# Fences between value steps as empty GpSimd instructions, and six instead of four bit transfers ahead of the first pair's fence

## The chip, the cores and the metric

The kernel runs on one core of a Trainium2 chip. The core has five engines with queues of their own: TensorE (PE, with its weight loads shown apart as PEld), VectorE (DVE), ScalarE (ACT), GpSimd (POOL) and SyncE (SP, which here only issues transfers). The metric is the device time of one execution in microseconds. Before the change it is 868.96 us, the median of three runs (868.72 to 869.63).

## What is computed

The reference is an attention with a mask from hashes, and behind it a feed-forward block. Cut to what matters:

```python
# q, k, v: (4, 8, 768, 64); proj: (64, 6); all float32
q_bucket = sum(((q @ proj) > 0) * 2**arange(6))      # six sign bits make a bucket; k the same
scores = where(q_bucket == k_bucket, q @ k.T / 8, -1e9)
attn = exp(scores - max) / (sum + 1e-9)
x = (attn @ v)                                        # brought to (3072, 512)
out = relu(x @ w_in)**2 @ w_out                       # 512 -> 2048 -> 512
```

Every query sees the keys whose six hash bits agree with its own.

## The kernel before

The kernel has an attention phase, up to about 320 us, and a feed-forward phase behind it (a fast product scheme by sums of blocks, with its weight sums prepared during the attention phase). The change touches the attention phase alone.

The 32 heads are worked off as 16 pairs, `for pr in range(NP)`. Two heads lie side by side on the 128 partitions, 64 each. The order of all instructions is written out by hand: on each engine the instructions run in the order in which the program names them.

For each pair the 768 keys are cut in six tiles `kt` of 128, and the 768 queries in two halves `i`. `score(pr, kt, i)` makes the scores of a key tile with a query half: `products` multiplies first the bits (`marks`), then the features, into one PSUM tile `st` (line 430), eight matmuls of 64 x 64; `weight` takes the exponential on ScalarE into a ring of four tiles `e` (line 436). A bit that differs subtracts so much that the exponential vanishes, which does the masking. `attend(pr, kt, s)` multiplies the weights with the values (`value`, line 486) and accumulates into `xo` in PSUM. `add_up` sums the weights on VectorE (line 473), and `sum_up` sums these over partitions with a matmul against ones (line 535). A step is one `score` and one `attend`; there are twelve in a pair, with `sum_up` and the hash products of the next pair (`hash_bits`, line 360) once in each.

The products with values are split by key halves (the upper and lower 64 rows of a key tile, multiplied side by side), and each `attend` has a parameter `s`: with `s` = 0 the first key half is multiplied with query half 0 and the second with query half 1, with `s` = 1 the other way round. Each query half has a PSUM block of its own, so at every change of `s` two key halves exchange the block into which they accumulate, and what the one has begun there must be finished before the other goes on. This is what `part(before, after)` does, the fence: a GpSimd instruction that waits for the last product before the change, and for which the first products behind the change wait. It is called in `attend` where `s` changes, and in `sum_up` between its halves: four times in an ordinary pair, ahead of `attend(pr, 0, 1)`, of `attend(pr, 2, 0)`, of `attend(pr, 4, 1)` (which runs in the next pair's turn) and of the second half of `sum_up`.

The instruction before the change is a write of one element into a tile `token` in SBUF (line 481). It waits for PE's semaphore, and, since all fences write the same element, for the write before it.

GpSimd also issues the transfers of the hash bits. `hash_bits` makes the products with `proj` for the next pair, `signs` and `weigh` turn them into signs and weights on ScalarE (tile `signed`), and `place_bits` (line 396) moves them to the partitions where `products` needs them, in eight transfers of 5.2 KB: four parts of (keys or queries, half), with two heads each. `PARTS` is the order of the parts: keys 0, queries 0, queries 1, keys 1. All eight are issued together behind `attend(pr, 0, 1)`, except for the first pair: there two parts are issued at that place, and the other two behind `attend(0, 2, 0)`, and so behind this one's fence on GpSimd's queue.

VectorE also converts weights for the feed-forward phase meanwhile, one piece a pair: `part_power` (line 151), `part_top` (lines 177 and 181), `round_weight` (lines 195 and 198), `sum_in` (line 594). `features` (line 344) transposes the next pair's queries and keys on VectorE.

The call of `place_bits` in the loop, ahead of `score(pr, 3, 1)`:

```python
            attend(pr, 0, 1)
            if more:
                place_bits(pr + 1, PARTS if pr else PARTS[:2])
```

Of the kernel before, what the change touches and what calls it, by code (L numbers as in the profile page):

```python
# [8 lines left out]
FP32 = mybir.dt.float32  # L9
# [25 lines left out]
def kernel(  # L35
# [10 lines left out]
    nc = tc.nc  # L46
# [50 lines left out]
    const = first.enter_context(tc.tile_pool(name="const", bufs=1))  # L97
# [11 lines left out]
    def spare(name):  # L109

        return ps_t.tile([P, 2, 512], FP32, name=name, tag="spare")
# [180 lines left out]
    def load_pair(pr):  # L292


        b, j = divmod(pr, PB)
        both = p_qk.tile([P, 2, S], FP32, name="qk_nat")
        for w, src in enumerate((q, k)):
            for g in range(4):
                h, e = divmod(g, 2)
                nc.sync.dma_start(  # L300
                    out=both[g * 32:(g + 1) * 32, w].rearrange("i (c d) -> i c d", d=32),
                    in_=src[b, 2 * j + h].rearrange("(c i) (e d) -> e i c d", i=32, e=2)[e],
                )
        nat[pr, "qk"] = both
# [36 lines left out]
    def features(pr):  # L341

        feat[pr] = p_f.tile([P, 2, S], FP32, name="feat")
        nc.vector.transpose(
            out=feat[pr].rearrange("p w s -> p (w s)"),
            in_=nat.pop((pr, "qk")).rearrange("p w s -> p (w s)"),
        )
# [39 lines left out]
    PARTS = (1, 0), (0, 0), (0, 1), (1, 1)  # L387

    def place_bits(pr, parts=PARTS):

        t = all_bits[pr % 2]
        for w, c in parts:
            bits[pr, w] = t[:, w]
            at = (2 * w + c) * NR_B
            for h in range(2):
                nc.gpsimd.dma_start(  # L396
                    out=t[h * D:h * D + NBITS + 1, w, c * HS:(c + 1) * HS],
                    in_=signed[at:at + NBITS + 1, h],
                )

    def first_keys(c, banks):

        if c == 0:
            bits[0, 1] = all_bits[0][:, 1]
        t = bits[0, 1]
        hash_bits(0, banks, (1,), (c,))
        at = slice((2 + c) * NR_B, (3 + c) * NR_B)
        cut = slice(c * HS, (c + 1) * HS)
        for h in range(2):
            nc.vector.tensor_scalar(  # L410
                out=t[h * D:h * D + NR_B, cut], in0=banks[at, h, 0:HS],
                scalar1=0.0, scalar2=None, op0=ALU.is_gt,
            )
        nc.vector.tensor_scalar(
            out=t[:, cut], in0=t[:, cut], scalar1=spans, scalar2=bases, op0=ALU.mult,
            op1=ALU.add,
        )
# [22 lines left out]
    def score(pr, kt, i, st=None):  # L440

        own = [feat[pr][:, w] for w in range(2)]
        marks = [bits[pr, w] for w in range(2)]
        st = st or turn("st")
        products(st, i, kt, marks, True)
        products(st, i, kt, own, False)
        weight(pr, kt, i, st)

    def first_score():

        own = [feat[0][:, w] for w in range(2)]
        marks = [bits[0, w] for w in range(2)]
        sts = [turn("st") for _ in range(2)]
        for i, st in enumerate(sts):
            products(st, i, 0, own, True)
        for i, st in enumerate(sts):
            products(st, i, 0, marks, False)
            weight(0, 0, i, st)
# [14 lines left out]
            nc.vector.tensor_tensor(out=totals[pr], in0=totals[pr], in1=e, op=ALU.add)  # L473

    SYNC = mybir.DependencyInfo(mybir.DependencyClass.Sync, mybir.DependencyReason.DATA)
    token = const.tile([1, 1], FP32, name="token")

    def part(before, after):


        step = nc.gpsimd.memset(token, 0.0)  # L481
        tc.add_manual_dep(step.ins, before.ins.name, SYNC)
        tc.add_manual_dep(after.ins, step.ins.name, SYNC)

# [7 lines left out]
    def attend(pr, kt, s):  # L492


        if (kt, s) == (0, 0):
            outs[pr] = ps_o.tile([P, 2, 512], FP32, name="xo")
        for r in range(2):
            for h in range(2):
                done = value(
                    pr, kt, slice(r * HK, (r + 1) * HK), h, (r + s) % 2,  # L500
                    (kt, s) == (0, 0), (kt, s) == (SB - 1, 1),
                )
                if turned.get(pr, s) != s:
                    part(lasts[pr], done)
                turned[pr] = s
        lasts[pr] = done
# [151 lines left out]
    with tc.manual_schedule():  # L658
# [21 lines left out]
        for pr in range(NP):  # L680
            more, old = pr + 1 < NP, pr - 1

            def beside(kt, s):
                if pr > 0:
                    attend(old, kt, s)

            if pr + 2 < NP:
                load_pair(pr + 2)
            if more and pr > 0:
                features(pr + 1)  # L690
            if pr == 0:
                first_score()
                first_keys(1, spare("hash"))
            else:
                score(pr, 0, 0)
                attend(old, 4, 0)
                score(pr, 0, 1)
                attend(old, 5, 0)
                add_up(old, SB - 1)
                if pr == 1:  # L700
                    part_top(0)
                round_weight(old)
                if later:
                    later.pop(0)()
                if more:
                    load_weight(pr + 1)
                for m in sums.get(pr, ()):
                    sum_in(m)
            score(pr, 1, 0)
            beside(4, 1)  # L710
            score(pr, 1, 1)
            beside(5, 1)
            if pr == 0:
                features(1)
            else:
                keep_x(old)
                sum_up(old, 0)
                if more:
                    hash_bits(pr + 1, turn("hash"))
                    signs(pr + 1)  # L720
                else:
                    score(pr, 2, 0)
                sum_up(old, 1)
                invert(old)
            add_up(pr, 1)


            if pr in (X_0 + 1, X_0 + 2):
                load_unit(pr - X_0 - 1)
            part_power(pr)  # L730
            if pr == 0:
                attend(pr, 0, 0)
            if more:
                score(pr, 2, 0)
            if pr > 0:
                spread(old)
                attend(pr, 0, 0)
            else:
                attend(pr, 1, 0)
            score(pr, 2, 1)  # L740
            if pr > 0:
                attend(pr, 1, 0)
                if more:
                    weigh()
                else:
                    place_power(pr, 0, 0)
            else:
                hash_bits(1, turn("hash"))
                signs(1)
            score(pr, 3, 0)  # L750
            if pr > 0:
                place_power(pr, 0, int(not more))
            else:
                weigh()
            attend(pr, 0, 1)
            if more:
                place_bits(pr + 1, PARTS if pr else PARTS[:2])
            score(pr, 3, 1)
            attend(pr, 1, 1)
            add_up(pr, 2)  # L760
            if pr > 0:
                normalize(old)
                if more:
                    place_power(pr, 0, 1)
                else:
                    place_power(pr, 1, 0)
            add_up(pr, 3)
            if more:
                load_values(pr + 1)


            score(pr, 4, 0)
            if more:
                place_power(pr, int(pr > 0), 0)
            else:
                place_power(pr, 1, 1)
            attend(pr, 2, 1)
            score(pr, 4, 1)
            if more:
                place_power(pr, int(pr > 0), 1)  # L780
            attend(pr, 3, 1)
            if 0 < pr < NP - 1:
                part_top(pr)
            score(pr, 5, 0)
            if pr == 0:
                place_power(0, 1, 0)
            if more:
                attend(pr, 2, 0)
            if pr == 0:
                place_bits(1, PARTS[2:])  # L790
            if 2 * PB < pr <= 2 * PB + NFT:
                load_x(0, slice(pr - 2 * PB - 1, pr - 2 * PB))
            score(pr, 5, 1, spare("st") if not more else None)
            attend(pr, 3, 0)
            if pr == 0:
                place_power(0, 1, 1)
            add_up(pr, 4)
        pr = NP - 1
# [810 lines left out]
```

## Time and profile before

| what | value |
|---|---|
| median of three runs | 868.96 us |
| the profiled execution | 869.21 us |
| its span (first to last instruction) | 867.3 us |
| PE busy | 854.5 us, 99% |
| DVE busy | 749.5 us, 86% |
| ACT busy | 361.9 us, 42% |
| POOL busy | 183.1 us, 21% |
| mean TensorE clock granted | 0.997 |
| writes of `token` on POOL | 62, together 14.6 us |
| bit transfers issued by POOL | 120, together 61.5 us |

Busy time is the time in which an engine had an instruction in work. In a row of the timeline stand the start, the duration, the engine, the line, the operation with what it writes and reads, and the count of instructions that were merged into the row; in brackets the idle time ahead of it and what ended it. In a row of a line or a tile stand the least, the median and the largest duration in ns. Weight loads (PEld) run ahead of the matmuls that use them, so that an idle PEld need not cost any time.

### The profile page before, as it was taken

How to read it: one execution, taken by the hardware profiler on the slowest of the kernel's cores; microseconds unless marked ns; L12 is line 12 of the kernel's file. 1: busy time of each engine (PE TensorE's matmuls, PEld its weight loads, DVE VectorE, ACT ScalarE, POOL GpSimd, SP SyncE). 2: the span in 40 equal slices, each digit the busy share in tenths (PEclk: the TensorE clock that was granted, in tenths of full speed). 3: DMA queues.
4: the chain of work that ended last, by engine and by line, in shares of the span. 5: the costliest groups of instructions: out<-in, count | busy, mean ns of one | idle time of the engine just before them, and what ended most of it. 6: DMA issues, size and time to landing. Idle time of an engine off the chain costs nothing.

```text
span 867.3 us, 16734 instructions
## 1 busy us (share of the span) xinstructions
PE 854.5 (99%) x6548; PEld 520.4 (60%) x6548; DVE 749.5 (86%) x1005; ACT 361.9 (42%) x648; POOL 183.1 (21%) x346
## 2 busy tenths in 40 slices
PE   8999999999999999999999999999999999999996
PEld 3544444444444444444788865557888655568885
DVE  5799999999999988998779978888889688888875
ACT  5787777788877752222111123332111233321110
POOL 1332222223322201652132111112000111100002
PEclk9999999999999999999999999999999999999998
DMA  9677899879998527999788865537758645355565
GB/s 206 127 139 151 177 176 203 192 168 249 249 222 223 167 68 258 319 308 298 279 287 258 187 158 175 171 112 254 260 150 189 158 168 170 117 167 160 147 182 100
DMA packets 226629, 168.03 MB, mean 194 GB/s; under 512 B 167112, under 2 KB 184848, under 8 KB 226544
## 3 DMA queue, kind: packets, MB, share of 16 engines
q1 hardware_dynamic: 187744, 87.19, 40.9%
q0 software_dynamic: 16416, 41.95, 15.7%
q10 hardware_dynamic: 22384, 37.76, 14.6%
q8 instruction: 53, 0.87, 0.4%
q14 instruction: 32, 0.26, 0.1%
HBM read 124.52 MB, written 41.68 MB: 192 GB/s over the span
## 4 chain that ended last, share of the span: by engine, by line
PE 96%; DMA 2%; DVE 1%; issue 0%; ACT 0%; POOL 0%; POOLq 0%; DVEq 0%; ACTq 0%
PE acc L837 39%; PE st L430 18%; PE acc L1056 16%; PE xo L486 14%; PE acc L1009 6%; PE tot L535 2%; PE hash L360 1%; DMA leaf<-w_out 1%; DMA bits<-signed 1%; PE xo L337 0%; DVE total L473 0%; PE tp L320 0%; POOL bits L396 0%; DVE bits L410 0%; ACT feat L327 0%
## 5 line engine op out<-in xcount | busy, mean ns | idle before, releaser
L436 ACT ACTIVATE e<-st 128x768 f32<-128x768 f32 x192 | 155.4, 810 | 62.4 <-PE st L430 59.2
L430 PE MATMUL st<-feat 64*64 64x384 f32 x1536 | 158.1, 483 | 1.0 <-DVE feat L329 1.0
L486 PE MATMUL xo<-e,v_nat 64*64 64x385 f32 (+1 forms) x1520 | 158.7, 485 | 0.0
L837 PE MATMUL acc<-b,leaf 128*128 128x256 f32 x600 | 133.4, 379 | 0.3 <-DMA leaf<-w_out 0.3
L837 PEld LDWEIGHTS acc<-b,leaf 128*128 128x128 f32 x600 | 113.6, 190 | 17.2 <-issue 1.4
L473 DVE TENSOR_TENSOR total<-total,e 128x1536 f32<-128x1536 f32 x64 | 111.8, 1746 | 4.4 <-ACT e L436 2.8
L486 PEld LDWEIGHTS xo<-e,v_nat 64*64 64x64 f32 (+1 forms) x1520 | 56.4, 133 | 69.9 <-issue 52.8
L1056 PE MATMUL acc<-t_x,w_unit 128*128 128x512 f32 x192 | 90.2, 592 | 0.0
L430 PEld LDWEIGHTS st<-feat 64*64 64x64 f32 x1536 | 57.3, 133 | 38.1 <-issue 33.5
L837 PE MATMUL acc<-t,leaf 128*128 128x256 f32 x336 | 76.2, 380 | 0.0
L837 PEld LDWEIGHTS acc<-t,leaf 128*128 128x128 f32 x336 | 63.7, 190 | 9.1 <-DVE t L594 0.5
L921 DVE SCALAR_TENSOR_TENSOR b<-h 128x512 f32<-128x512 f32 x96 | 65.7, 691 | 3.0
L430 PE MATMUL st<-bits 64*64 64x384 bf16 x768 | 65.8, 325 | 1.1 <-DMA bits<-signed 1.0
L396 POOL DMA_DIRECT2D bits<-signed x120 | 61.5, 520 | 23.2 <-ACT signed L385 22.8
L1056 PE MATMUL acc<-x,w_unit 128*128 128x512 f32 x128 | 60.1, 592 | 0.0
L481 POOL MEMSET token<- 1x1 f32 x62 | 14.6, 236 | 206.0 <-PE xo L486 155.9
L837 PE MATMUL acc<-x,w_unit 128*128 128x512 f32 x128 | 56.5, 593 | 0.0
L1056 PEld LDWEIGHTS acc<-t_x,w_unit 128*128 128x128 f32 x192 | 36.5, 190 | 28.9 <-issue 26.8
L837 PE MATMUL acc<-b_t,leaf 128*128 128x256 f32 x240 | 53.8, 379 | 0.0
L1154 POOL DMA_DIRECT2D out_dram<-h x26 | 16.8, 654 | 174.1 <-DVE h L1147 167.1
L874 POOL DMA_DIRECT2D raw_qk<-in_q_dram x32 | 17.3, 541 | 162.4 <-DVE peaks L878 162.4
L837 PEld LDWEIGHTS acc<-b_t,leaf 128*128 128x128 f32 x240 | 45.5, 190 | 6.2
(156 smaller groups left out, 1206.6 us busy)
## 6 DMA issues: line engine op xcount, KB each, us to landing
leaf<-w_out ACTq DMA_DIRECT2D x142, 256.0 KB, 3.2
w_unit<-w_in SPq DMA_DIRECT2D x16, 640.0 KB, 4.0
raw<-in_moe_w_in_dram SPq DMA_DIRECT2D x8, 1024.0 KB, 6.8
raw<-in_moe_w_out_dram SPq DMA_DIRECT2D x8, 1024.0 KB, 7.4
w_unit<-w_in SPq DMA_DIRECT2D x8, 896.0 KB, 8.6
w_out<-sums POOLq DMA_DIRECT2D x16, 448.0 KB, 7.9
sum<-w_in SPq DMA_DIRECT2D x16, 448.0 KB, 5.0
v_nat<-in_v_dram SPq DMA_DIRECT2D x16, 384.0 KB, 5.3
```

Source lines behind the costliest of these rows:

```text
L396: nc.gpsimd.dma_start(out=t[h * D:h * D + NBITS + 1, w, c * HS:(c + 1) * HS], in_=signed[at:at + NBITS + 1, h],)
L430: nc.tensor.matmul(out=st[k * HK:(k + 1) * HK, h, 0:HS], lhsT=src[1][rows, key], rhs=src[0][rows, cut], start=first, stop=not first, skip_ ...
L436: nc.scalar.activation(out=key_of(pr, kt)[:, :, i, 0:HS], in_=st[:, :, 0:HS], func=ACTF.Exp, scale=scale)
L473: nc.vector.tensor_tensor(out=totals[pr], in0=totals[pr], in1=e, op=ALU.add)
L486: return nc.tensor.matmul(out=outs[pr][h * D:(h + 1) * D, c, 0:HS + 1], lhsT=nat[pr, "v_nat"][rows, h, kt * D:(kt + 1) * D], rhs=key_of(pr ...
L535: done = nc.tensor.matmul(out=spares[pr][g * 32:(g + 1) * 32, c2, 0:QS], lhsT=ones[rows], rhs=totals[pr][rows, h, c, c2 * QS:(c2 + 1) * QS ...
L837: nc.tensor.matmul(out=acc[to], lhsT=a(i), rhs=b(i), start=first and i == 0, stop=last and i == n - 1, skip_group_check=True,)
L874: nc.gpsimd.dma_start(out=raw_qk[i][:, w], in_=flat[:, i * n:(i + 1) * n])
L921: nc.vector.scalar_tensor_tensor(out=out, in0=h, scalar=0.0, in1=h, op0=ALU.max, op1=ALU.mult)
L1009: nc.tensor.matmul(out=out, lhsT=w[:, a], rhs=b, start=start, stop=stop, skip_group_check=True)
L1056: nc.tensor.matmul(out=acc[to], lhsT=w[:, PLACE[a], f], rhs=bt[b](f), start=first and f == 0, stop=last and f == NFT // 2 - 1, skip_group_ ...
L1154: queue.dma_start(out=out[at, m0 + a * 32:m0 + (a + 1) * 32].rearrange("(c i) j -> i c j", i=32), in_=ot[a * 32:(a + 1) * 32].rearrange("i ...
```

## The change

The fence becomes an empty GpSimd instruction (`nop`) with the same two dependences, and the tile `token` goes. For the first pair, three of the four parts of the bits (six transfers) are issued at the earlier place instead of two (four transfers), so that one part remains behind the fence of `attend(0, 2, 0)`.

```diff
     SYNC = mybir.DependencyInfo(mybir.DependencyClass.Sync, mybir.DependencyReason.DATA)
-    token = const.tile([1, 1], FP32, name="token")
 
     def part(before, after):
-        step = nc.gpsimd.memset(token, 0.0)
+        step = nc.gpsimd.nop()
         tc.add_manual_dep(step.ins, before.ins.name, SYNC)
         tc.add_manual_dep(after.ins, step.ins.name, SYNC)
...
             attend(pr, 0, 1)
             if more:
-                place_bits(pr + 1, PARTS if pr else PARTS[:2])
+                place_bits(pr + 1, PARTS if pr else PARTS[:3])
             score(pr, 3, 1)
...
                 attend(pr, 2, 0)
             if pr == 0:
-                place_bits(1, PARTS[2:])
+                place_bits(1, PARTS[3:])
```

In the built program the empty instruction is a semaphore step of GpSimd's sequencer with a semaphore of its own. Five of the eight bit transfers of each later pair get one more semaphore step ahead of them (a wait for matmuls that read the same bits tile two pairs earlier). On the other engines the order of the instructions is as before.

## The prediction

> **What bounds the kernel now.** I read the page first (busy time, the chain that ended last, the costliest groups), then the answers for the tile `token` and for line 396, then the timeline around single fences, at last the busy time of each engine over whole pairs.
>
> ```profile
> PE 854.5 (99%) x6548; PEld 520.4 (60%) x6548; DVE 749.5 (86%) x1005; ACT 361.9 (42%) x648; POOL 183.1 (21%) x346
> ...
> PE 96%; DMA 2%; DVE 1%; issue 0%; ACT 0%; POOL 0%; POOLq 0%; DVEq 0%; ACTq 0%
> ...
> L481 POOL MEMSET token<- 1x1 f32 x62 | 14.6, 236 | 206.0 <-PE xo L486 155.9
> L481 POOL MEMSET token<- x62: 88/89/563, 17.5 to 314.5; 1x1 f32 x62
>   PEld xo L486: 16.7, 45
> ```
>
> PE is the bound: 99% busy, 96% of the chain. POOL is on the chain for under half a per cent, so 14.6 us of one-element writes say nothing yet. What matters is only where a late fence made PE start late. The third and fourth rows already show the oddity: 62 writes of one element take from 88 to 563 ns. The last row says that weight loads for value products waited 16.7 us for them; weight loads run ahead of the products, so most of that may be free.
>
> The timeline tells which fences are not free. A step of the attention phase is a group of score products and then a group of value products; its length is the distance from one `st<-bits` row to the next.
>
> ```profile
> 44.02 0.33 PE L430 MATMUL st<-bits 64*64 64x384 bf16 x4
> 44.82 0.82 PE L486 MATMUL xo<-e,v_nat 64*64 64x385 f32 x8
> 45.47 0.33 PE L430 MATMUL st<-bits 64*64 64x384 bf16 x4
> 45.62 0.69 DVE L177 TENSOR_SCALAR top<-raw 128x1024 uint32<-128x1024 uint32 x1
> 45.81 0.54 POOL L481 MEMSET token<- 1x1 f32 x1 [0.17 <-PE xo L486]
> 46.40 0.21 PEld L486 LDWEIGHTS xo<-e,v_nat 64*64 64x64 f32 x8 [0.62 <-POOL token L481]
> 46.40 0.88 PE L486 MATMUL xo<-e,v_nat 64*64 64x385 f32 x8
> 47.09 0.34 PE L430 MATMUL st<-bits 64*64 64x384 bf16 x4
> 48.55 0.34 PE L430 MATMUL st<-bits 64*64 64x384 bf16 x4
> ```
>
> 44.02 to 45.47 is 1.45 us, 47.09 to 48.55 is 1.46, but 45.47 to 47.09 is 1.62: this step lost 0.17 us. The fence between the two value groups began at 45.81 and ended at 46.35, and the products behind it started at 46.40. The vector operation of line 177 ran from 45.62 to 46.31, so the write ended just behind it.
>
> This is the fence in front of `attend(pr, 2, 0)`, the second of four in each pair. The other three cost nothing:
>
> ```profile
> 39.53 0.69 DVE L151 TENSOR_SCALAR power<-raw 128x1024 uint32<-128x1024 uint32 x1
> 39.65 0.33 PE L430 MATMUL st<-bits 64*64 64x384 bf16 x4
> 39.98 0.27 POOL L481 MEMSET token<- 1x1 f32 x1 [3.88 <-PE xo L486]
> 40.31 0.30 PEld L486 LDWEIGHTS xo<-e,v_nat 64*64 64x64 f32 x8 [0.35 <-POOL token L481]
> 41.11 0.33 PE L430 MATMUL st<-bits 64*64 64x384 bf16 x4
> ...
> 51.79 0.09 POOL L481 MEMSET token<- 1x1 f32 x1 [5.45 <-PE xo L486]
> 51.94 0.15 PEld L486 LDWEIGHTS xo<-e,v_nat 64*64 64x64 f32 x4 [0.17 <-POOL token L481]
> ...
> 285.79 0.09 POOL L481 MEMSET token<- 1x1 f32 x1 [3.35 <-PE tot L535]
> ```
>
> The first fence took 0.27 us, also ending with a vector operation (39.53 + 0.69 = 40.22 against 40.25), yet its step is 39.65 to 41.11, the usual 1.46: 0.33 us from the start of the write to the weight load is absorbed. The third took 0.09. The fourth (in front of the second half of the sums, line 535) takes 0.09 as well (285.79). The stall returns in each of the pairs 1 to 14; the last:
>
> ```profile
> 293.79 0.33 PE L430 MATMUL st<-bits 64*64 64x384 bf16 x4
> 295.24 0.33 PE L430 MATMUL st<-bits 64*64 64x384 bf16 x4
> 295.58 0.53 POOL L481 MEMSET token<- 1x1 f32 x1 [0.17 <-PE xo L486]
> 296.87 0.34 PE L430 MATMUL st<-bits 64*64 64x384 bf16 x4
> ```
>
> 1.45 us, then 1.63. The total fits: 14 writes of 0.54, 14 of 0.28 and 34 of 0.09 make 14.5 of the 14.6 us. Pairs 0 and 15 have none of the long ones.
>
> **The change part by part.** *Removed: 62 writes; added: 62 empty instructions.* In the built program an empty instruction is one step of POOL's sequencer: it waits for PE and counts up a semaphore of its own, for which PE then waits. It touches no memory. The trace has no such row; nearest are POOL's own semaphore steps and the short writes.
>
> ```profile
> L396 POOLq EVENT_SEMAPHORE  x16: 17/17/43, 21.8 to 289.8; - x16
> L396 POOL DMA_DIRECT2D bits<-signed x120: 512/518/674, 22.5 to 294.9; - x120
>   PE st L430: 1.0, 1
> DMA to landing us min/median/max: 1.5/3.7/5.9
> ...
> 22.46 2.22 POOL L396 DMA_DIRECT2D bits<-signed  x4 [4.91 <-ACT signed L385]
> 25.28 0.09 POOL L481 MEMSET token<- 1x1 f32 x1 [0.60 <-PE xo L486]
> 25.42 0.16 PEld L486 LDWEIGHTS xo<-e,v_nat 64*64 64x64 f32 x4 [0.16 <-POOL token L481]
> 25.76 2.05 POOL L396 DMA_DIRECT2D bits<-signed  x4 [0.39 <-issue]
> 29.02 0.66 PE L430 MATMUL st<-bits 64*64 64x384 bf16 x4 [0.99 <-DMA bits<-signed]
> 41.55 4.09 POOL L396 DMA_DIRECT2D bits<-signed  x8 [1.29 <-ACT signed L385]
> ```
>
> Lower end 0.02 us, upper end 0.09, the write at 51.79 that nothing disturbed. Both ends give the same sum, since even 0.27 (39.98) cost PE nothing: the stall of 0.17 goes whole. 14 x 0.17 = 2.4 us. The other 48 fences give nothing, because there PE is hidden from them by the score products that it still has in hand; without that cover the first fence would cost up to 0.17 us a pair today. What is late next at this place: nothing, the products are in order behind the score products of 45.47.
>
> Why the write took 0.54 us has two readings: the vector operation beside it, or the eight transfers whose descriptors POOL had just finished. The fence at 39.98 had no transfers before it since 27.81 (25.76 + 2.05) and still ended with the vector operation, so I take the first. The Trainium skill says the same in "SBUF — State Buffer", section "SBUF: two separate sides": VectorE and GpSimd share one port pair as an exclusive lock, and the one that comes second waits for the whole instruction. By that rule an instruction without memory never waits and the sum is the 2.4 us above; by the other reading an empty instruction could still be held behind the transfers, and the sum would be 0.
>
> *Waits added to the transfers.* The write counted as POOL's own work, and the transfers behind it took over its knowledge of PE's progress; the empty instruction counts apart, so five of the eight transfers of each pair get a semaphore step of their own ahead of them, for PE products of two pairs ago, long done. Queued behind them on POOL is the second fence, and PE behind that. Price: 5 x 0.02 us = 0.1 at the least, if none overlaps; the upper end is 5 x 0.09 = 0.45.
>
> Four transfers without such steps took 2.05 us (0.51 each); eight with two such steps among them took 4.09, also 0.51 each. So they hide under the 0.5 us of a transfer, and I take 0. Even the 0.45 would put the end of the eight from 45.64 to 46.09, still ahead of today's 46.35.
>
> *Six transfers ahead of the first pair's fence instead of four.* Two transfers (the queries' second half) move from behind the fence of 25.28 to 24.68, where the first four end; they are issued 1.08 us earlier, and the last two then also come 1.08 us earlier, at 25.70. Past the fence the order on POOL is otherwise the same, no other queue is touched. Gain: PE waits for bits once, 0.99 us at 29.02, but that is for the first four, which stay where they are; the two moved ones were not waited for (`PE st L430: 1.0, 1` is the only wait for any of them). Loss: the fence is queued behind two more transfers, 25.70 instead of 25.28 if it must wait for their end, and PE's weight load of 25.42 with it. That would cost at most what the later fence at 46.40 costs, 0.17 us, once. Whether a sequencer step waits for the end of POOL's work ahead of it isn't in these rows. In the Trainium skill's "PSUM — Partial Sum Buffer", section "Engine vs sequencer instructions", a sequencer waits only until earlier instructions are handed to the engine; by that the fence is on time and the cost 0. I take 0 and keep 0.17.
>
> The first four share engines with two more in flight, so their landing may shift either way. In the chain it is one row:
>
> ```profile
> 23.65 5.23 DMA bits<-signed
> ```
>
> At the slowest landing of any such transfer, 5.9 us, PE would start 0.7 us later; at the best the whole wait goes, 1.0 us. The moved ones stand behind the four in the same queue, so I take 0 between −1.0 and +0.7.
>
> **The sum.** The profiled execution took 869.21 us for a span of 867.3. 869.21 − 2.4 = 866.8; it stands 0.25 above the median of the three runs, so 868.96 − 2.4 gives 866.5.
>
> **The rivals.** *VectorE takes the gain.* In these pairs it is nearly as full as PE:
>
> ```profile
> core 0: us, PE busy (x) PEld busy (x) DVE busy (x) ACT busy (x) POOL busy (x), PEclk, DMA share, GB/s
> 189.73:208.95 19.22, 19.22 (x304) 9.06 (x288) 18.91 (x19) 14.96 (x24) 5.71 (x14) 1.00 0.95 237
> 208.95:228.16 19.21, 19.21 (x304) 9.09 (x288) 18.39 (x18) 14.96 (x24) 5.64 (x14) 1.00 1.01 241
> ```
>
> A pair of 19.21 us becomes 19.04. The ordinary pair needs 18.4 of VectorE, every third 18.9: both still fit, with 0.1 us to spare in the worst. If VectorE held all fourteen pairs at 19.21, the time would stay 868.96; if it held three pairs as full as the first row, 0.5 comes back: 867.0.
>
> *The empty instruction is no cheaper.* If it is held behind the transfers as the second reading has it, 868.96. Against it speaks 39.98.
>
> *The added waits slow POOL's queue: slower.* The second fence stands behind them. Its place today is 46.35; each transfer slower by d moves it to 45.64 + 5d. It decides from 5d = 0.7, that is 0.14 us a transfer. At 0.25 the fence would be at 46.89, 0.54 us behind today's in each of 14 pairs: 868.96 + 7.6 = 876.5. Steps of 17 to 43 ns speak against it, and the equal pace of 0.51.
>
> *The first pair's transfers land otherwise.* 865.5 with the whole wait gone, 867.2 with 0.7 more.
>
> **How the numbers follow.** Full gain with the first pair as it is: 0.58, 866.5, own range 866.0 to 867.1. First pair better as well: 0.09. First pair worse: 0.08, half of it still under 867.2. VectorE or the empty instruction keep most of the gain: 0.17, 867.3 to 869.2. Slow queue: 0.08. What a measurement of this kernel can tell is about 0.2%, 1.7 us, so faster means below 867.2: 0.58 + 0.09 + 0.04 = 0.71; within 0.2% 0.04 + 0.17 = 0.21; slower 0.08. The range 865.3 to 868.9 holds the first three cases and most of the fourth.
>
> **What would show it.** The step behind the second fence is 1.45 us in pairs 1 to 14, a pair from sum fence to sum fence is 19.04, no weight load of the value products waits 0.6 us for a fence. The eight transfers still take 4.1 us. In pair 0 the products at 25.73 are on time, and PE's wait at 29.02 is about 1 us. Wrong would be: a fence answered later than 46.1 in its pair, pairs still at 19.21 with VectorE without a pause, or a later landing of the first four bits.

## The result and the profile after

The kernel after takes 866.67 us (median; 865.79 to 868.13), beside 869.27 us for the kernel before on the same chip: a ratio of 0.9971, 95% interval 0.996 to 0.9982. The forecast was 866.5. Beside the last experiments it was measured again: 867.05 against 869.64, ratio 0.9973 (0.9961 to 0.9984). Both times the change is worth 2.6 us. The profiled execution took 866.6 us.

From the page of the kernel after: span, busy times, and the chain that ended last.

```profile
span 864.4 us, 16743 instructions
PE 851.6 (99%) x6548; PEld 519.3 (60%) x6548; DVE 749.3 (87%) x1005; ACT 362.3 (42%) x648; POOL 169.4 (20%) x284
...
PE 95%; DMA 2%; DVE 1%; issue 0%; POOL 0%; ACT 0%; POOLq 0%; DVEq 0%; ACTq 0%
```

POOL lost 13.7 us of work and its 62 writes. PE's busy time fell by 2.9 us though it does the same products: before, the stalls counted as busy (19.21 of 19.21 us in a pair).

The answers for line 480 (the fence, now a step of POOL's sequencer) and for the transfers:

```profile
L480 POOLq EVENT_SEMAPHORE  x62: 17/17/17, 17.0 to 311.2; - x62
  PEld xo L485: 7.8, 44
L396 POOL DMA_DIRECT2D bits<-signed x120: 515/521/677, 22.0 to 291.9; - x120
L396 POOLq EVENT_SEMAPHORE  x87: 17/17/43, 21.4 to 290.4; - x87
```

A fence takes 17 ns everywhere, and weight loads wait 7.8 us for it where they waited 16.7 us for the write. The transfers have 87 semaphore steps instead of 16, and a transfer takes 521 instead of 518 ns.

The timeline at the fence that the prediction was about:

```profile
43.40 0.33 PE L430 MATMUL st<-bits 64*64 64x384 bf16 x4
44.85 0.33 PE L430 MATMUL st<-bits 64*64 64x384 bf16 x4
45.01 0.69 DVE L177 TENSOR_SCALAR top<-raw 128x1024 uint32<-128x1024 uint32 x1
45.34 0.14 PEld L485 LDWEIGHTS xo<-e,v_nat 64*64 64x64 f32 x4 [0.18 <-POOLq L480]
46.30 0.33 PE L430 MATMUL st<-bits 64*64 64x384 bf16 x4
```

The same vector operation runs from 45.01 to 45.70 beside the fence, and the weight load starts at 45.34, in the middle of it. The step is 44.85 to 46.30, 1.45 us, where it was 1.62.

Two whole pairs, each as long as from one sum fence to the next (the same two as in the prediction; columns are the stretch, its length, busy time and instructions of each engine):

```profile
187.64:206.67 19.03, 19.03 (x304) 8.97 (x292) 18.81 (x20) 14.97 (x24) 4.72 (x9) 1.00 0.93 237
206.67:225.70 19.03, 19.03 (x304) 8.97 (x292) 18.40 (x18) 14.97 (x24) 4.66 (x9) 1.00 1.00 243
```

A pair has shrunk from 19.21 to 19.03 us. The thirteen pairs 2 to 14, from the first product of pair 2 to that of pair 15, took 249.77 us in the profile before and 247.39 in the one after: 2.38 us. The spans of the two profiles differ by 2.9 us. Of the rest, 0.45 us lie ahead of the first product of the phase and 0.34 in the pairs 0 and 1; the feed-forward phase is 0.3 us longer.

The first pair, where the transfers were moved:

```profile
22.02 4.33 POOL L396 DMA_DIRECT2D bits<-signed  x8 [18.06 <-ACT signed L385]
24.96 0.17 PEld L485 LDWEIGHTS xo<-e,v_nat 64*64 64x64 f32 x4 [0.15 <-POOLq L480]
25.29 0.84 PE L485 MATMUL xo<-e,v_nat 64*64 64x385 f32 x8
28.71 0.35 PE L430 MATMUL st<-bits 64*64 64x384 bf16 x3 [0.46 <-DMA bits<-signed]
```

The products behind the fence start on time at 25.29, in the midst of POOL's row of transfers. PE still waits for the first pair's bits; all in all that step and the next lose 1.22 us here, where they lost 1.39 before.

### The profile page after: what moved, and what is told of

It is laid out like the page before. It is cut to its first block, busy times and chain, and to the rows that moved or that the text cites. A ratio compares the mean times of both kernels' runs of the same rounds, so it can differ in the third digit from the quotient of the medians.

```text
span 864.4 us, 16743 instructions
## 1 busy us (share of the span) xinstructions
PE 851.6 (99%) x6548; PEld 519.3 (60%) x6548; DVE 749.3 (87%) x1005; ACT 362.3 (42%) x648; POOL 169.4 (20%) x284
## 4 chain that ended last, share of the span: by engine, by line
PE 95%; DMA 2%; DVE 1%; issue 0%; POOL 0%; ACT 0%; POOLq 0%; DVEq 0%; ACTq 0%
PE acc L836 39%; PE st L430 17%; PE acc L1055 16%; PE xo L485 14%; PE acc L1008 6%; PE tot L534 2%; PE hash L360 1%; DMA leaf<-w_out 1%; DMA bits<-signed 1%; DVE bits L410 0%; DVE feat L344 0%; DVE total L473 0%; POOL bits L396 0%; DVE total L468 0%; PE xo L360 0%
## 5 line engine op out<-in xcount | busy, mean ns | idle before, releaser
L843 ACT COPY two<-acc 128x256 f32<-128x256 f32 (+1 forms) x29 | 12.5, 432 | 87.8 <-PE acc L836 78.4
```

## The experiments

Step lengths below are read as in the prediction, from one `st<-bits` row to the next, and "pair" means from sum fence to sum fence. Free of stalls, a step is 1.454 us and a pair 19.03. Between single executions of one of these kernels lie up to 6.6 us, more than most of the effects, so steps and pairs of the profiles carry the argument and the medians are held against them.

### The two halves of the change, each alone

Empty instructions at all fences, with the first pair's transfers as before:

```diff
-        step = nc.gpsimd.memset(token, 0.0)
+        step = nc.gpsimd.nop()
```

> The empty instruction in all fences, but four transfers of the first pair ahead of its fence as before. Theory (only the write of the second fence cost anything, 0.17 us in each of 14 pairs): 2.4 us less than before, the steps behind the second fence at 1.45 us, pairs from sum fence to sum fence at 19.02 to 19.04 us; PE waits about 1 us for the first pair's bits, as before. Rival (part of the gain is the two moved transfers): clearly less than 2.4 us gained, and the first pair's wait is the difference.

Measured: 867.04 us beside 869.42, ratio 0.9977 (0.9968 to 0.9987). Steps behind the second fence 1.454 us, pairs 19.03: the whole gain.

The writes kept, six transfers ahead of the first pair's fence:

```diff
-                place_bits(pr + 1, PARTS if pr else PARTS[:2])
+                place_bits(pr + 1, PARTS if pr else PARTS[:3])
...
-                place_bits(1, PARTS[2:])
+                place_bits(1, PARTS[3:])
```

> The writes are kept, six transfers ahead of the first pair's fence. Theory: within 0.3 us of before, pairs at 19.21 us, the second fence's write still about 0.54 us long. If the first pair's fence must wait for the sixth transfer's end, its write starts at about 25.7 us instead of 25.3 and the step behind it is up to 0.2 us longer. Rival (the moved transfers bring the bits earlier): up to 1.0 us less than before.

Measured: 869.49 us, ratio 0.9995 (0.9986 to 1.0003). Pairs stay at 19.21. Its first pair in the timeline:

```profile
22.64 3.25 POOL L396 DMA_DIRECT2D bits<-signed  x6 [4.91 <-ACT signed L385]
25.11 0.36 PE L430 MATMUL st<-bits 64*64 64x384 bf16 x4
25.89 0.09 POOL L481 MEMSET token<- 1x1 f32 x1
26.73 0.34 PE L430 MATMUL st<-bits 64*64 64x384 bf16 x4
```

A write has to wait for the end of the six transfers (22.64 + 3.25 = 25.89), and its step is 25.11 to 26.73, 1.62 us: the 0.17 us that the prediction kept as an upper end. The empty instruction in the kernel after passed at the start of the sixth transfer and cost nothing.

What the moved transfers are worth is seen in the profile of the empty instructions alone, where the fifth and sixth stand behind the fence:

```profile
29.03 0.11 PEld L430 LDWEIGHTS <-bits 64*64 64x64 bf16 x2 [0.45 <-DMA bits<-signed]
29.85 0.35 PE L430 MATMUL st<-bits 64*64 64x384 bf16 x3 [0.47 <-DMA bits<-signed]
```

Here the first four had landed in time, and the step at 29.06 waited for the fifth and sixth (landed at 28.99 and 29.81), 0.69 us in all. So the order matters when the first four happen to be early. How early they are changes with each execution: the loss at this place was 1.39 us in the profile before, 1.22 and 0.96 in two of the kernel after, 1.57 in one of the last runs, and nothing in that of the six transfers alone.

### The second fence alone, and all others alone

```diff
-    def part(before, after):
-        step = nc.gpsimd.memset(token, 0.0)
+    def part(before, after, empty=False):
+        step = nc.gpsimd.nop() if empty else nc.gpsimd.memset(token, 0.0)
...
-                    part(lasts[pr], done)
+                    part(lasts[pr], done, s == 0)
```

`s == 0` is `attend(pr, 2, 0)`. The other kernel has `s != 0` there and `empty=True` as the default.

> Only the fence ahead of attend(pr, 2, 0) is empty, the other three of each pair stay writes; four transfers ahead as before. Theory: the same gain as with all of them empty, 2.4 us, since the other 46 cost PE nothing. Rival (every fence costs a little, in proportion to the time that weight loads waited for it): about a quarter of the gain, 0.6 us.

> The opposite: the fence ahead of attend(pr, 2, 0) stays a write, the other three are empty. Theory: no gain (within 0.3 us of before), the step behind the second fence still 1.62 us, the write still about 0.54 us. Rival (every fence costs): about 1.8 us gained.

Measured: the second fence alone 867.9 us, ratio 0.9978 (0.9969 to 0.9987), steps behind that fence 1.454 in all fourteen pairs, pairs 19.03 where nothing else stalls. The other 46 alone 869.29, ratio 0.9996 (0.9987 to 1.0005), steps behind the second fence 1.62 us and more. The answers for the tile `token`, of the first and then of the second:

```profile
L481 POOL MEMSET token<- x46: 89/89/522, 17.4 to 307.6; 1x1 f32 x46
```

```profile
L481 POOL MEMSET token<- x16: 88/532/546, 25.2 to 313.3; 1x1 f32 x16
```

In the kernel before, three quarters of the fences cost nothing, and one in four all of it. Even the 0.01 us by which the sum step became shorter (3.020 to 3.010) goes with the second fence.

With the second fence alone empty, one thing changes for the others. In the pairs 6, 9 and 12 of its profile the first fence, still a write, comes late:

```profile
134.78 0.33 PE L430 MATMUL st<-bits 64*64 64x384 bf16 x4
134.91 0.69 DVE L151 TENSOR_SCALAR power<-raw 128x1024 uint32<-128x1024 uint32 x1
135.12 0.51 POOL L481 MEMSET token<- 1x1 f32 x1 [3.88 <-PE xo L486]
136.38 0.34 PE L430 MATMUL st<-bits 64*64 64x384 bf16 x4
```

The write ends at 135.63, behind the vector operation of line 151 (until 135.60), and the step is 1.60 us. These three steps lost 0.43 us together. In the kernel before, the same three writes took 0.32 to 0.36 us and cost nothing. So the first fence, free in the kernel before, is not free in every pair once the second one no longer stalls. With all fences empty this loss does not appear. The medians (867.9 here, 867.04 with all fences empty) don't resolve 0.4 us.

### The vector operation elsewhere, with the writes kept

What holds the write, the vector operation beside it or the transfers ahead of it? Here the kernel before keeps its writes, and line 177's operation is issued one place earlier on VectorE, ahead of an `add_up`, so that it lies beside transfers instead of beside the fence (the operation moves into a helper, which is called there):

```diff
-            out=top, in0=high, scalar1=0xFFFFF, scalar2=0x100000,
+            out=top, in0=raws[i][:, :, :, 1], scalar1=0xFFFFF, scalar2=0x100000,
...
+            if 0 < pr < NP - 1 and pr in parts:
+                early[pr] = top_first(pr)
```

> The kernel before, all fences writes, but the first vector operation of part_top (line 177 of before) stands one place earlier on VectorE, ahead of add_up(pr, 3), so that the sum (two inputs, line 473) and not the one-input operation lies beside the second fence. Theory (the write waits for the one-input vector operation that runs beside it): the second fence's write falls from 0.54 to about 0.09 us although the eight transfers still end just ahead of it, the step behind it is 1.45 us, and the gain is 2.4 us with writes in all fences. Rival (the write is slow because POOL has just written eight transfers' descriptors): 0.54 us and no gain.

Measured: 868.09 us beside 869.12, ratio 0.9987 (0.9976 to 0.9998). Its timeline (lines are 8 higher here, so the fence is line 489):

```profile
97.27 4.22 POOL L404 DMA_DIRECT2D bits<-signed  x8 [1.29 <-ACT signed L393]
99.67 0.70 DVE L177 TENSOR_SCALAR top<-raw 128x1024 uint32<-128x1024 uint32 x1
101.18 0.33 PE L438 MATMUL st<-bits 64*64 64x384 bf16 x4
101.52 0.09 POOL L489 MEMSET token<- 1x1 f32 x1
102.64 0.33 PE L438 MATMUL st<-bits 64*64 64x384 bf16 x4
```

The write comes 0.03 us behind the eight transfers (97.27 + 4.22 = 101.49) and still takes 0.09 us. In all fourteen pairs this write takes 0.09 us, and the step is 1.46 at most. That refutes the transfers as the cause. A vector operation still runs beside the write, the sum of line 481 (line 473 of the kernel before), but it has two inputs and does not hold it.

The price of line 177 has not gone altogether: the transfers beside it take 4.22 instead of 4.09 us, but nobody waits for that. And the gain is 1.0 us by the medians, not the 2.4 expected. In the profile the thirteen pairs took 248.32 us, 1.45 less than before; of the missing 0.93, 0.44 lie in the first fence of the pairs 6, 9 and 12, as with the second fence alone, 0.32 in one late landing of bits and 0.12 in the sum step behind it. The profiled execution took 866.94 us; why the median is 1.15 us above it is not known.

### A wide write ahead of the second fence

This puts a POOL write of 128 x 512 elements, which nothing reads, ahead of the second fence, once with the empty instruction and once with the one-element write:

```diff
                 if turned.get(pr, s) != s:
+                    if s == 0:
+                        nc.gpsimd.memset(busy, 1.0)
                     part(lasts[pr], done)
```

> The changed kernel with a write of 128 x 512 bf16 (nothing reads it) on POOL ahead of the second fence of each pair. Theory (the empty instruction is a step of the sequencer, which goes on once the earlier instruction is handed over): no change of time against the changed kernel, 866.7 us, the fence is answered while the write still runs. Rival (the step waits for the end of POOL's work ahead of it): the write ends at about 46.2 us where the products want to start at 45.7, so 0.5 us or more in each of 14 pairs, 7 us slower than the changed kernel.

> The kernel before with the same write of 128 x 512 bf16 ahead of the second fence. The fence is a write itself and comes behind it. Theory: the added write waits for the vector operation of line 177, ends about 0.45 us behind it, and the fence behind that; PE's step is 0.6 to 0.8 us longer than 1.45 instead of 0.17, so 6 to 9 us slower than before. It is the control for the run with the empty instruction: if this one is not slower, that one tells nothing.

Measured with the empty instruction: 867.99 us, ratio 0.9984 (0.9972 to 0.9996), steps 1.454, pairs 19.03. The timeline of one fence, and two rows of another pair:

```profile
100.85 0.33 PE L430 MATMUL st<-bits 64*64 64x384 bf16 x4
101.01 1.11 DVE L177 TENSOR_SCALAR top<-raw 128x1024 uint32<-128x1024 uint32 x1
101.03 0.54 POOL L504 MEMSET busy<- 128x512 bf16 x1
101.34 0.14 PEld L485 LDWEIGHTS xo<-e,v_nat 64*64 64x64 f32 x4 [0.18 <-POOLq L480]
102.31 0.33 PE L430 MATMUL st<-bits 64*64 64x384 bf16 x4
...
196.46 1.11 POOL L504 MEMSET busy<- 128x512 bf16 x1
196.49 0.14 PEld L485 LDWEIGHTS xo<-e,v_nat 64*64 64x64 f32 x4 [0.18 <-POOLq L480]
```

The weight load starts at 101.34, while POOL's write runs until 101.57. At 196.49 it starts 1.08 us ahead of the end of a write that was itself held. So an empty instruction does not wait for the end of POOL's work ahead of it.

With the one-element write: 869.17 us, ratio 1.0002 (0.9986 to 1.0018). I had expected it 6 to 9 us slower, the wide write and then the fence each behind the vector operation. It went otherwise:

```profile
102.52 0.33 PE L430 MATMUL st<-bits 64*64 64x384 bf16 x4
102.67 1.11 DVE L177 TENSOR_SCALAR top<-raw 128x1024 uint32<-128x1024 uint32 x1
102.69 0.55 POOL L505 MEMSET busy<- 128x512 bf16 x1
103.15 0.09 POOL L481 MEMSET token<- 1x1 f32 x1
103.31 0.21 PEld L486 LDWEIGHTS xo<-e,v_nat 64*64 64x64 f32 x8 [0.48 <-POOL token L481]
104.01 0.34 PE L430 MATMUL st<-bits 64*64 64x384 bf16 x4
```

The wide write took its own 0.55 us, and the vector operation lasted 1.11 instead of 0.69. This time VectorE was the one held, although its record starts 0.02 us earlier. The one-element write then took 0.09 us and the step 1.49 us, shorter than the 1.62 of the kernel before. The time came out unchanged all the same: the first fence's writes of the pairs 6, 9 and 12 took 0.67 to 0.69 us and their steps lost 0.3 us each, and the sum steps of the pairs 3 and 10 lost 0.2 to 0.3.

So this run is not the control that I meant it to be. What shows that the empty step doesn't wait are the rows at 101.34 and 196.49, not the two times.

### More empty steps ahead of each transfer

The slower rival said that steps added to the transfers push the second fence back on POOL's queue. To price it, the kernel after gets n empty steps ahead of every transfer from the second pair on, for which the transfer waits:

```diff
+                steps = []
+                for _ in range(n if pr > 1 else 0):
+                    steps.append(nc.gpsimd.nop())
+                    tc.add_manual_dep(steps[-1].ins, lasts[pr - 2].ins.name, SYNC)
-                nc.gpsimd.dma_start(
+                move = nc.gpsimd.dma_start(
...
+                for step in steps:
+                    tc.add_manual_dep(move.ins, step.ins.name, SYNC)
```

First n = 4:

> The changed kernel with four more empty steps and one more wait ahead of each bit transfer from the second pair on. Theory (such steps are done while the engine writes the descriptors of the transfer ahead, 0.5 us each): transfers still 0.52 us apart, time within 0.3 us of the changed kernel. Rival (they add to the transfers): five steps of 0.07 to 0.1 us each, 0.35 to 0.5 us a transfer, the second fence 2.8 to 4 us later and the time 30 us or more above the changed kernel.

Measured: 887.2 us, ratio 1.0203 (1.0185 to 1.0221), 20.5 us slower than the kernel after by the median of its first measurement. That they would hide was wrong. The last two transfers of a pair and the fence:

```profile
107.25 0.52 POOL L400 DMA_DIRECT2D bits<-signed  x1 [0.33 <-POOLq L398]
108.09 0.52 POOL L400 DMA_DIRECT2D bits<-signed  x1 [0.33 <-POOLq L486]
108.15 0.88 PE L491 MATMUL xo<-e,v_nat 64*64 64x385 f32 x8 [1.51 <-POOLq L486]
```

Transfers start 0.84 to 0.87 us apart instead of 0.52, and each of them still takes 0.52: the steps add to the distance. Their records lie in the first 0.35 us of the transfer ahead (102.986 to 103.281 beside the one that starts at 102.930), and the next transfer starts 0.52 us behind the last of them, at 103.799. The fence (line 486) fires as the last transfer starts, too late, and PE is idle for 1.51 us. With n = 1 and n = 2 the question was whether there is a slack:

> The kernel after with one more empty step ahead of each transfer from the second pair on (four more gave a pace of 0.869 us a transfer instead of 0.521, and 20.5 us in 14 pairs, 1.46 us a pair). Theory with a slack: steps past the free one cost 0.078 us each, so the pace is 0.869 - 3 x 0.078 = 0.635 us and the second fence 8 x 0.114 = 0.91 us later; four more steps put it 2.78 us later and cost 1.46, so 1.32 us are free: no change, 866.6 and second steps of 1.454 us. Rival without slack (the cost goes with the number of steps): a quarter of 20.5, 5.1 us slower, about 871.7.

> The kernel after with two more empty steps ahead of each transfer from the second pair on. Theory with a slack: pace 0.713 us, the fence 8 x 0.192 = 1.54 us later, 0.22 us past the slack of 1.32: 14 x 0.22 = 3.0 us slower than the kernel after, about 869.6, with second steps of about 1.7 us. Rival without slack: half of 20.5, 10.2 us slower, about 876.8.

Measured for n = 1: 869.3 us beside 869.64, ratio 0.9995 (0.9983 to 1.0008), 2.2 us slower than the kernel after of that session (867.05). The timeline around one fence:

```profile
98.90 4.91 POOL L400 DMA_DIRECT2D bits<-signed  x8 [14.13 <-POOLq L398]
102.82 0.33 PE L436 MATMUL st<-bits 64*64 64x384 bf16 x4
103.34 0.43 PEld L491 LDWEIGHTS xo<-e,v_nat 64*64 64x64 f32 x8 [0.22 <-POOLq L486]
104.27 0.33 PE L436 MATMUL st<-bits 64*64 64x384 bf16 x4
```

The eight transfers take 4.91 instead of 4.15 us, and the step behind the fence is 1.45 all the same: 0.76 us are free. It is so in eleven of the fourteen pairs; in the other three single transfers took longer and the step lost 0.06 to 0.35 us. Yet the thirteen pairs took 1.72 us more than in the kernel after of the same session (249.11 against 247.39). Of that 1.37 us lie in three pairs in which bits landed only when their products were due (in one at 202.88 us, the rest of its products starting at 202.93). Whether the steps made them late is not shown: one such wait of 0.2 to 0.7 us stands also in the profiles of the second fence alone, of the vector operation elsewhere and of the next load later, which have no added steps. My forecast of no change was mostly right on the fence and had left out what else may wait behind the steps.

For n = 2: 871.76 us, ratio 1.0024 (1.0015 to 1.0034), 4.7 us slower than the kernel after. The timeline:

```profile
103.96 0.33 PE L436 MATMUL st<-bits 64*64 64x384 bf16 x4
105.03 0.21 PEld L491 LDWEIGHTS xo<-e,v_nat 64*64 64x64 f32 x8 [0.77 <-POOLq L486]
105.73 0.34 PE L436 MATMUL st<-bits 64*64 64x384 bf16 x4
```

The steps behind the second fence are now 1.77 us, 0.32 more than free of stalls (2.07 in two of the fourteen pairs); 14 x 0.32 = 4.5 of the 4.7 us. A cost in proportion to n would have been 10.2; a slack of 1.32 us would have given 3.0. That slack came from eight times the pace, and the rows of eight grew less than that: from 4.15 us to 4.91, 5.46 and 6.55 with n = 1, 2 and 4. For n = 2 that is 1.31 us more, less the 0.32 that PE lost; for n = 4 it is 2.40, less 1.41. Both leave a slack of 1.0 us.

### The next load later

A try at a better version: in the kernel after, the load of the second pair's values, and what SyncE has queued behind it, waits for the last product of `attend(0, 2, 0)`, so that less moves beside the first pair's bits.

```diff
+                load_values(1)
+                tc.add_manual_dep(held[0].ins, lasts[0].ins.name, SYNC)
```

> The kernel after, with the load of the second pair's values (and the loads queued behind it on SyncE) held until the last product of the first pair's first stage, at about 26.2 us of the span. In the profiles so far TensorE waited for the first pair's bits 1.22 us in the kernel after, 0.69 us with the empty instructions alone, 1.41 us with the second fence alone, and not at all in four others. Theory (the bits' landing in pair 0 is late because other loads share the DMA engines with them): the wait goes in every execution, 0.3 to 0.9 us faster than the kernel after run beside it, about 866.1. Rival (the spread comes from elsewhere, the feed-forward stage for one): as the kernel after, within 0.3 us. A loss of more than 0.5 us would say that the held load is then itself too late for the second pair.

> The kernel after once more, beside the three others. By its pairs of 19.02 instead of 19.21 us it stands 2.4 to 2.6 us under the kernel before: 866.6, with executions up to 1 us to either side by the first pair's wait for its bits and by the waits of the feed-forward stage.

Measured: 866.54 us (865.59 to 867.21) against 867.05 (865.56 to 869.87) for the kernel after beside it; ratios to the kernel before 0.9963 (0.9949 to 0.9977) and 0.9973 (0.9961 to 0.9984). In its profile PE does not wait for the first pair's bits, as the theory has it, and the 0.5 us between the medians is of the size expected. But the intervals overlap, and other kernels had profiles without that wait and no held load. Whether it beats the kernel after stays open.

## Why the prediction was right

**Only the second fence costs: right, with its size.** 0.17 us x 14 = 2.4 us was the term. Measured: 0.168 us at that step and 0.01 at the sum step, 2.5 us for 14 pairs, and 2.38 in the thirteen that were compared whole. In the kernel before only the second fence costs PE anything. That nothing is late next held for the change as a whole, but not for the second fence alone: there the first fence's write cost 0.14 to 0.15 us in three pairs.

**The write waited for the vector operation: right.** With line 177's operation moved away, the same write behind the same transfers takes 0.09 us. The other reading is out. It is not any vector operation that holds the write. The write at 51.79, which I called undisturbed, had one beside it:

```profile
50.94 1.72 DVE L473 TENSOR_TENSOR total<-total,e 128x1536 f32<-128x1536 f32 x1
```

It took 0.09 us beside this sum of two inputs; only beside the one-input operations of the lines 151 and 177 did writes become long. The two wide writes show the same lock from its other side: there the vector operation is held, 1.11 us instead of 0.69. The Trainium skill, "SBUF — State Buffer", section "SBUF: two separate sides", calls it an exclusive lock, and 0.54 us for one element agrees. By that section the first to start has the port; by the records here the vector operation started 0.02 us ahead and yet was held, so the recorded starts don't tell who came first when they lie this close. Where the vector operation started 0.06 us ahead (at 196.40, beside the wide write of 196.46) it took its 0.71 us, and the write lasted 1.11.

**VectorE as the next bound: did not come.** Its pairs went down with PE's, to 19.03 us with 18.81 of work in the fullest.

**The added waits: the price was right, the reason was not.** I took 0 because steps "hide under the 0.5 us of a transfer". The change's own five waits cost 4.15 − 4.09 = 0.06 us a pair: transfers with such a wait start 0.522 us apart instead of 0.509, 0.013 for each, which indeed nobody feels. But steps don't hide as such: with n = 1, eight empty steps and three more waits cost 0.76 us a pair, and thirty-two empty steps 2.40. From n = 1 to 2 each empty step adds 0.078 us (0.635 to 0.713 us a transfer), so a wait alone is far cheaper than an empty instruction; why, I can't say from these runs. My evidence for hiding was also thin: of the two steps in the row at 41.55 one had passed at 39.99, ahead of its first transfer. Nor was the point of decision right. I had the fence behind the end of the eight transfers, so that 0.14 us for each of five waits, 0.7 us in all, would bring it to the old place. An empty step passes when the last transfer starts, half a microsecond earlier, so 0.76 us cost most steps nothing and even 1.31 us cost only 0.32. The slower rival is a real mechanism; with 0.06 us a pair this change stayed more than a factor of ten below the 1.0 us that were free.

**Six transfers ahead of the first pair's fence: right at this fence.** The upper end of 0.17 us is what a write pays there, and the empty instruction pays 0. The page "PSUM — Partial Sum Buffer" of the Trainium skill, section "Engine vs sequencer instructions", says that a sequencer waits only until earlier work is handed over; the weight load at 101.34 beside a POOL write that ran until 101.57 agrees.

**"The two moved ones were not waited for": only true of the profile before.** In another execution they were what PE waited for, 0.69 us. The loss at this place goes from 0 to 1.6 us with the same code there; against the 1.39 us of the profile before that is −1.4 to +0.2, where I had allowed −1.0 to +0.7, since I had counted the idle time of 0.99 us alone. That it averages to nothing for this change is supported by the two medians with and without the move (866.67 and 867.05 against 867.04), not shown more finely than some tenths.

**What is not accounted for:** kernels whose undisturbed pairs are 19.03 us had medians from 866.5 to 868.1. The waits for the first pair's bits (0 to 1.6 us by profile), single late bits around pair 10 (0.2 to 0.7 us), the first fences of three pairs and single pauses of PE in the feed-forward phase (up to 2.1 us, for which the profile names no cause) are seen, but which of them made which median was not tried.

## What to carry to other kernels

An instruction that exists only to order two others should touch no memory: a write of one element on GpSimd can wait for the end of a vector operation beside it (here those with one input, not the sums of two). Look for the few places where such an ordering step is late, by step lengths and not by its total time: here 14 of 62 fences carried the gain, and the rest were covered by products that PE still had in hand. Such cover can go when the first stall goes, so look again with that one mended. Such an empty step tells nothing of the end of its own engine's earlier work, so it may stand only for waits that it makes itself, as these fences do for PE's products.

## What the runs showed of the hardware

- An empty GpSimd instruction takes 17 ns on the sequencer, and the weight load behind it starts while a POOL write of 0.54 us or a transfer of 0.52 us is still in work.
- The lock between VectorE and GpSimd holds either: a one-element write lasts 0.54 us beside a 0.69 us vector operation with one input, and that operation lasts 1.11 us beside a 0.55 us write. Beside a sum of two inputs of 1.72 us the one-element write takes 0.09 us.
- Eight transfers issued beside the same vector operation took 4.22 us instead of 4.09. Only the one that was in work when the operation ended became longer: 0.65 us instead of 0.52 (99.81 to 100.46), until 0.10 us behind the end of the operation (100.37).
- Empty steps ahead of a GpSimd transfer lengthen the row of eight transfers, on the average by 0.07 us for each added step or wait (0.76 us for eleven, 1.31 for nineteen, 2.40 for thirty-five), though the transfer itself stays at 0.52 us.
